# A fused attention and two-expert-layer kernel: background steps of the weights spread by phase, and four PSUM banks for one product

## The chip, the cores and the metric

The kernel runs on one core of a Trainium2 chip. The metric is the device time of one execution in microseconds (us). TensorE (PE) has two levels of clock here, 1.2 and 2.4 GHz; the profile gives the granted share of the higher one. VectorE is called DVE, ScalarE ACT; SP only issues DMAs here.

## The reference

```python
kv  = einsum('bhsd,bhse->bhde', k, v)            # 4 batches, 8 heads, 576 tokens, head size 64
o   = einsum('bhsd,bhde->bhse', q, kv)
x   = o / sqrt(mean(o*o) + 1e-6) * g             # -> 2304 tokens x 512

p   = domain_probs / domain_probs.sum(-1)        # first layer: 4 experts, every token in every one
for e in range(4):
    out += p[:, e] * (relu(x @ w1[e]) @ w2[e])   # 512 -> 1024 -> 512

logits = out @ phi                               # second layer: 8 experts with 4 slots each
d = softmax(logits, over tokens); c = softmax(logits, over slots)
y = c @ [relu((d.T @ out)[e] @ w1'[e]) @ w2'[e] for e in range(8)]
```

All inputs are float32. Most of the arithmetic is the first layer: two products for each of 4 experts over 2304 tokens.

## The kernel before, in words

The 2304 tokens are 18 tiles of 128. Tiles make chunks: chunk 0 is tiles 0 to 3, chunk 1 tiles 4 to 7, and so on, the last one with two tiles. Chunks 0 and 1 are group 0 and go through experts 0, 1, 2, 3 first; chunks 2 to 4 then go through experts 3, 2, 1, 0. The change touches group 0.

A float32 matrix is held as two float16 halves, hi and lo (`split`, L615: ACT writes hi at L618 with a scale, DVE writes lo = scaled source - hi at L620), and each product is three matmuls, hi*hi, hi*lo and lo*hi. The first product of a chunk (`mm1`, L908) goes by seven products of 2x2 block operands instead of eight, so the weight operands include differences of blocks, T1 to T4, made on DVE (L655). The second product has two forms: plain (`mm2`, L979, one PSUM bank of 128x512 per tile, at the end of a tile one DVE instruction at L1004 scales the bank and adds it to the running sum) and fast (`mm2_fast`, L1011, again seven products, with sums of 128x256 pieces added at L1045). The fast form needs differences of the hidden activations (lines 837 to 886; they are queued by `fast_h` and worked off about one a step by `work_off`, L819) and of w2's blocks (made at L738, `prep_t2`).

For experts 1 and 2 in group 0 (`SOON`) an expert has four phases: first product of chunk 0 (plain), first product of chunk 1 (feeding the fast form), plain second product of chunk 0, fast second product of chunk 1. Expert 0 is plain throughout and goes chunk by chunk.

The order of instructions is written out by hand. `main` is a list of steps (12 matmuls of 256 columns or 6 of 512 each); a first product has 14 steps, chunk 0's second 16, chunk 1's fast second 14. Beside each step, `run_bg` (L1366) takes steps from background chains. A chain has a start, an end and a list of steps, and gives each main step a weight: 1, or W1 = 0.55 for a step of a first product, and 0 for the two steps before a second product and its first step (`CALM`). Its steps are dealt out in proportion. Two chains matter here. In phases of expert e - 1, `prep_w1` and `prep_w2` prepare expert e: four size steps on ACT (L541) for w1, then `scale_steps` (a reduce and a small diagonal matrix on DVE at L548 and L553, empty steps, a tiny matmul `ar_w` on PE at L561, small DVE steps), 15 steps of splits and differences of w1, then the same for w2 with 9 steps of splits. `prep_t2` prepares w2's differences of the expert itself, with 8 differences at L738 and 8 splits, in two batches that are also written to DRAM.

PSUM has eight banks in four pools of two: `ps_x`, `ps_o`, `ps_yz`, `ps_a`. A step of the main list names its pool: in chunk 0's second product of experts 1 and 2 all four tiles take turns on the two banks of `own` (`ps_x`), while `other` (`ps_o`) is lent to the background's small matmuls; chunk 1's fast product that follows starts its products 1 and 7 in the two banks of `ps_o`.

SP issues the DMAs of its own queue in program order; an input page is loaded when a page is free and not claimed, at most ten at a time (`pump`, L169).

Of the kernel before, what the change touches and what calls it, by code (L numbers as in the profile page):

```python
# [43 lines left out]
W1 = 0.55  # L44
# [3 lines left out]
def attn_moe_softmoe_kernel(ctx: ExitStack, tc: tile.TileContext, qT, k, v, g, dp, w1, w2, phi, m1, m2a, m2b, out):  # L48
# [442 lines left out]
    def pe(f):  # L491
        after[0].append(f)
# [25 lines left out]
    def attn_steps(cs, eng, stride=6):  # L518

        ps_ = [p for c in cs for p in pairs(c)]  # L520
        st = [[] for _ in range(stride * (len(ps_) - 1) + len(pair_steps(ps_[0], eng)))]
        for i, p in enumerate(ps_):
            for j, f in enumerate(pair_steps(p, eng)):
                st[i * stride + j].append(f)
        return [lambda fs=fs: [f() for f in fs] for fs in st]
# [19 lines left out]
    def w_scale_a(e, nm, act=False):  # L545
        m = wmx.pop((e, nm))
        a = small.tile([128, 1], F32, tag=f"am{nm}", name=f"am_{nm}_{e}")
        nc.vector.tensor_reduce(out=a, in_=m, axis=AX.X, op=ALU.add)  # L548
        dg = work.tile([128, 128], F32, tag="dgw", name=f"dg_{nm}_{e}")
        if act:  # L550
            nc.scalar.activation(dg, gdiag, AF.Copy, scale=a)
        else:
            nc.vector.tensor_scalar(  # L553
                out=dg, in0=gdiag if nm == "w1" else ident, scalar1=a, scalar2=None, op0=ALU.mult
            )
        war[e, nm] = dg

    def w_spread(e, nm, bank=ps_a, between=lambda: None):

        ps = bank(f"ar_{nm}_{e}")  # L560
        nc.tensor.matmul(ps[:, 0:128], ones, war[e, nm], start=True, stop=True)  # L561
        between()
        r = war[e, nm] = small.tile([128, 1], F32, tag=f"ar{nm}", name=f"ar_{nm}_{e}")
        nc.vector.tensor_reduce(out=r, in_=ps[:, 0:128], axis=AX.X, op=ALU.add if nm == "w1" else ALU.max)

    def scale_steps(e, nm):

        return [lambda: w_scale_a(e, nm), lambda: None, lambda: None, lambda: pe(lambda: w_spread(e, nm)),
                lambda: w_scale_b(e, nm)]

    def w_scale_b(e, nm, between=lambda: None):
# [185 lines left out]
    def prep_w2(g_, e):  # L757
        raw = lambda b: need(("w2", g_, e, b))
        st = []
        if g_ == 0:  # L760
            st += [lambda b=b: w_size(e, "w2", b) for b in range(4)]
            st += scale_steps(e, "w2")

        def sp(b, i, part):
            w2_split(e, b, b, i, part)

        bi = [(b, i) for b in (0, 2, 1, 3) for i in range(2)]
        return st + stagger(
            [lambda b=b, i=i: sp(b, i, 0) for b, i in bi], [lambda b=b, i=i: sp(b, i, 1) for b, i in bi]
        )  # L770
# [501 lines left out]
    is1 = []  # L1272
# [15 lines left out]
    for e, seq in runs:  # L1288
        if True:
            for n, (gi, which, c) in enumerate(seq):  # L1290
                ei = EXP[gi].index(e)
                wk = (0 if e == KEPT else gi, e)
                last = gi == 1 and ei == E - 1
                kept = gi == 0 and e == KEPT
                soon = gi == 0 and e in SOON
                fast = c != 0 if e == KEPT or soon else gi == 1 and not (last and c == DISP[-1])
                turns = gi == 1 or e == KEPT or soon

                own, other = (ps_x, ps_o) if n % 2 == 0 else (ps_o, ps_x)
                ch = CH[c]  # L1300
                marks[f"mm{which}", gi, e, c] = len(main)
                done = not kept and not any(i == which for g_, i, _ in seq[n + 1:])
                if which == 1:
                    if not turns:
                        own, other = ps_x, ps_o
                    st = [lambda wk=wk, c=c, u=u, P=P, fast=fast, bank=own: mm1(wk, c, u, P, fast, bank)
                          for P in ORDER for u in range(2)]
                    if not fast:
                        st[0] = lambda c=c, f=st[0]: (start_chunk(c), f())
                    if ei == E - 1:  # L1310
                        st[-1] = lambda c=c, f=st[-1]: (f(), x_drop(c))
                    if done:
                        st[-1] = lambda wk=wk, f=st[-1]: (f(), [pg.release() for pg in wop[wk].values()])
                    if not fast:
                        st[-1] = lambda f=st[-1]: (f(), flush())
                elif fast:
                    st = [lambda wk=wk, c=c, P=P, j=j, bank=own, ei=ei: mm2_fast(wk, c, P, j, bank, ei == 0)
                          for P in ORDER3 for j in range(len(ch) // 2)]
                    st[-1] = lambda wk=wk, c=c, f=st[-1]: (f(), end_fast(wk, c))
                    if done:  # L1320
                        st[-1] = lambda wk=wk, f=st[-1]: (f(), [pg.release() for pg in w2p[wk].values()])
                else:

                    tu = [(ch[0], 0), (ch[1], 0), (ch[0], 1), (ch[1], 1)] + [(t, u) for t in ch[2:] for u in range(2)]
                    st = [
                        lambda wk=wk, c=c, t=t, u=u, kk=kk, ei=ei, b=own if soon else ps_o:
                        mm2(wk, c, t, u, kk, ei == 0, b)
                        for t, u in tu for kk in range(2)
                    ]
                    if last and done:  # L1330

                        st = []
                        for u in range(2):
                            for kk in range(2):
                                st += [
                                    lambda wk=wk, c=c, t=t, u=u, kk=kk, b=(ps_w if t in ch[2:] else ps_o):
                                    mm2(wk, c, t, u, kk, False, b) for t in ch
                                ]
                                st[-1] = lambda wk=wk, c=c, u=u, kk=kk, f=st[-1]: (
                                    f(), hbuf[c][2 * u + kk].release(), w2p[wk][2 * kk + u].release()  # L1340
                                )
                    else:
                        st[-1] = lambda c=c, f=st[-1]: (f(), end_chunk(c))
                        if done:
                            st[-1] = lambda wk=wk, f=st[-1]: (f(), [pg.release() for pg in w2p[wk].values()])
                main += st
                is1 += [which == 1] * len(st)
                lend += [other if which == 1 or fast or soon else ps_w] * len(st)
                marks["end" if which == 2 else "mm1end", gi, e, c] = len(main)


# [8 lines left out]
    def chain(start, stop, steps, claim=0, w1=W1):  # L1360
        assert start < stop
        hooks.setdefault(start, []).append(lambda: (
            chains.append([start, stop, deque(steps), w1, 0.0, []]), claims.__setitem__(0, claims[0] + claim)
        ))

    def run_bg(now):  # L1366

        for ch in chains:
            start, stop, steps, w1, credit = ch[:5]
            wt = [(w1 if is1[i] else 1.0) * calm[i] for i in range(now, stop)]  # L1370
            if not wt:
                n = len(steps)
            else:
                credit += wt[0] * (len(steps) - credit) / max(sum(wt), 1e-3)
                n = min(int(credit + 1e-6), max(1, -(-len(steps) // len(wt))))
                ch[4] = credit - n
            for _ in range(min(n, len(steps))):
                for f in ch[5]:
                    f()
                ch[5].clear()  # L1380
                after[0] = ch[5]
                steps.popleft()()
# [15 lines left out]
    chain(6, m["mm2", 0, 0, 0], w2s[4:-4], 4)  # L1398
    chain(m["mm2", 0, 0, 0] - 2, m["mm2", 0, 0, 0] + 4, w2s[-4:])
    chain(10, m["mm1", 0, 0, 1], attn_steps([1], nc.vector), 3 + 6, 1.0)  # L1400
    for e in range(1, E):
        chain(m["mm2", 0, 0, 0] + 12 if e == 1 else m["mm1", 0, e - 1, 0], m["end", 0, e - 1, 1] - 1,
              prep_w1(0, e, V) + prep_w2(0, e), 12 if e == 1 else 6)
    def claim(at, n):
        hooks.setdefault(at, []).append(lambda: claims.__setitem__(0, claims[0] + n))

# [6 lines left out]
    chain(m["end", 0, E - 1, 1] + 3, m["end", 1, E - 1, 2], disp_steps(1), 2, 1.0)  # L1413
    for e in FAST:
        if e in SOON:
            chain(m["mm1", 0, e, 0] + 2, m["mm2", 0, e, 1] - 2, prep_t2(e, V), 2)
        else:
            chain(m["mm1", 1, E - 1, 4], m["mm2", 1, E - 1, 4], prep_t2(e, V), 4)
            gate["w2", 1, e] = m["mm1", 1, E - 1, 4] - 6
        gate[e] = m["mm1", 1, e + 1, 3]  # L1420
# [435 lines left out]
```

## Time and profile before

| | us |
|---|---|
| three runs | 824.14, 824.60, 825.47 |
| profiled execution, its own time | 825.78 |
| its span, first to last instruction | 824.0 |
| PE busy | 801.3 (97%) |
| DVE busy | 571.2 (69%) |
| ACT busy | 398.5 (48%) |
| mean granted PE clock | 0.993 |

The span is what the trace covers; 1.8 us of the execution's time lie around it. Matmuls are pipelined, so PE's busy time says only that it seldom waits; the shares of DVE and ACT are means over stages that differ.

### The profile page before, as it was taken

What the parts mean: (1) busy time and instruction counts of PE and PEld (TensorE: products, weight loads), DVE (VectorE), ACT (ScalarE), POOL (GpSimd) and SP (SyncE); (2) the same over time, 40 slices, a digit from 0 to 9 for tenths busy, and PEclk for the clock granted to TensorE, in tenths of its full rate; (3) what the DMA queues carried; (4) which work ended last, traced back from release to release, by engine and by line L of the source; (5) the groups of instructions that cost most, each with busy time, mean ns of one, the idle gap of its engine ahead of it and who ended that gap; (6) DMA issues with size and microseconds to landing.
All of it is one profiled execution on the core that took longest, in us unless ns stands there. A gap on an engine that the chain in (4) does not pass through costs nothing.

```text
span 824.0 us, 17838 instructions
## 1 busy us (share of the span) xinstructions
PE 801.3 (97%) x7558; PEld 644.8 (78%) x7558; DVE 571.2 (69%) x1139; ACT 398.5 (48%) x784; POOL 5.9 (1%) x13
## 2 busy tenths in 40 slices
PE   8999999999999999999999999999999999999996
PEld 8876668658855876878888888898889888984545
DVE  6997967987798557769969727874578537742403
ACT  5876756555655333774656536241444125421203
POOL 0000000000000000000000000000000000000000
PEclk9999999999999999999999999999999999999998
DMA  9951540277228600110012860044103252669697
GB/s 361 403 238 50 198 189 27 77 258 264 102 68 287 248 28 1 51 29 2 1 52 85 306 251 1 1 181 141 66 1 115 92 204 82 227 226 362 216 395 234
DMA packets 40753, 126.03 MB, mean 153 GB/s; under 512 B 4066, under 2 KB 11106, under 8 KB 40674
## 3 DMA queue, kind: packets, MB, share of 16 engines
q1 hardware_dynamic: 40016, 124.57, 41.6%
q8 instruction: 59, 0.97, 0.5%
q10 hardware_dynamic: 658, 0.33, 0.1%
q14 instruction: 20, 0.16, 0.1%
HBM read 96.57 MB, written 28.31 MB: 152 GB/s over the span
## 4 chain that ended last, share of the span: by engine, by line
PE 83%; DVE 13%; ACT 2%; issue 2%; DVEq 0%; POOL 0%; ACTq 0%; POOLq 0%
PE p L929 33%; PE m L1029 25%; PE y L992 13%; DVE pages L620 3%; PE s L1705 2%; PE o L339 2%; PE so L1735 2%; PE keep L264 1%; DVE pages L946 1%; DVE t L959 1%; PE kv L284 1%; PE x2T L1062 1%; DVE pages L738 1%; DVE pages L844 1%; PE xT L408 1%
## 5 line engine op out<-in xcount | busy, mean ns | idle before, releaser
L929 PE MATMUL p<-pages 128*128 128x256 f16 (+1 forms) x3360 | 339.4, 262 | 1.5 <-DVE kvs L308 1.0
L929 PEld LDWEIGHTS <-pages 128*128 128x128 f16 x3360 | 300.0, 98 | 34.7 <-issue 2.1
L1029 PE MATMUL m<-pages 128*128 128x256 f16 x2016 | 224.7, 273 | 2.3 <-DVE pages L1045 2.3
L1029 PEld LDWEIGHTS <-pages 128*128 128x128 f16 x2016 | 196.9, 98 | 26.8 <-issue 3.9
L992 PE MATMUL y<-pages 128*128 128x512 f16 x576 | 132.0, 386 | 5.4 <-DVE pages L1004 4.6
L992 PEld LDWEIGHTS <-pages 128*128 128x128 f16 x576 | 56.9, 100 | 72.4 <-issue 10.6
L1045 DVE SCALAR_TENSOR_TENSOR pages<-m,pc,pages 128x256 f32<-128x256 f32 x148 | 65.8, 480 | 63.1 <-PE m L1029 62.6
L618 ACT ACTIVATE pages<-pages,s_w 128x512 f16<-128x512 f32 (+1 forms) x113 | 79.4, 740 | 20.9 <-DVE s_w L594 16.0
L620 DVE SCALAR_TENSOR_TENSOR pages<-pages,s_w 128x512 f16<-128x512 f32 (+1 forms) x113 | 85.1, 778 | 3.1 <-ACT pages L618 2.8
L839 ACT CAST pages<-t 128x512 f16<-128x512 f32 (+1 forms) x84 | 46.5, 557 | 57.5 <-DVE t L882 24.1
L848 DVE TENSOR_TENSOR pages<-t,pages 128x512 f16<-128x512 f32 (+1 forms) x84 | 50.5, 608 | 2.5 <-ACT pages L839 1.3
L837 ACT ACTIVATE pages<-pages 128x512 f16<-128x512 f32 (+1 forms) x56 | 31.9, 569 | 35.6 <-DVE pages L871 19.1
L959 DVE TENSOR_TENSOR t<-p,t 128x512 f32<-128x512 f32 x36 | 24.7, 689 | 25.7 <-PE p L929 25.5
L839 ACT CAST pages<-pages 128x512 f16<-128x512 f32 (+1 forms) x28 | 15.6, 558 | 53.3 <-DVE t L886 53.3
L945 ACT ACTIVATE pages<-t 128x512 f16<-128x512 f32 x36 | 22.6, 628 | 30.1 <-DVE t L959 29.8
L867 DVE TENSOR_TENSOR t<-p,t 128x512 f32<-128x512 f32 (+1 forms) x28 | 17.1, 613 | 26.2 <-PE p L929 25.2
L871 DVE TENSOR_TENSOR pages<-p,pages 128x512 f32<-128x512 f32 (+1 forms) x28 | 17.1, 612 | 25.5 <-PE p L929 25.5
L541 ACT ACTIVATE junk<-pages 128x1024 bf16<-128x1024 f32 x32 | 33.8, 1055 | 2.2 <-DMA pages<-in_w 1.8
L954 ACT COPY t<-p 128x512 f32<-128x512 f32 x36 | 20.8, 579 | 28.4 <-PE p L929 28.4
L844 DVE SCALAR_TENSOR_TENSOR pages<-pages 128x512 f16<-128x512 f32 (+1 forms) x56 | 33.1, 608 | 0.9 <-ACT pages L837 0.5
L861 ACT COPY t<-p 128x512 f32<-128x512 f32 (+1 forms) x28 | 14.5, 525 | 39.4 <-PE p L929 39.4
L946 DVE SCALAR_TENSOR_TENSOR pages<-t,pages 128x512 f16<-128x512 f32 x36 | 24.6, 684 | 1.1 <-ACT pages L945 0.7
(184 smaller groups left out, 699.0 us busy)
## 6 DMA issues: line engine op xcount, KB each, us to landing
pages<-in_w SPq DMA_DIRECT2D x48, 512.0 KB, 4.6
o<-pages SPq DMA_DIRECT2D x33, 512.0 KB, 7.6
pages<-o SPq DMA_DIRECT2D x33, 512.0 KB, 6.1
pages<-in_m SPq DMA_DIRECT2D x32, 512.0 KB, 5.3
pages<-in_m2a SPq DMA_DIRECT2D x16, 512.0 KB, 5.3
pages<-in_m2b SPq DMA_DIRECT2D x16, 512.0 KB, 10.1
o_t<-pages SPq DMA_DIRECT2D x12, 512.0 KB, 5.0
pages<-o_t SPq DMA_DIRECT2D x12, 512.0 KB, 5.4
```

What stands on the lines that cost most here:

```text
L541: nc.scalar.activation(junk, src, AF.Square if nm == "w1" else AF.Abs, accum_out=m[:, b:b + 1])
L618: nc.scalar.activation(dst[:, 0], src, AF.Copy, scale=s)
L620: nc.vector.scalar_tensor_tensor(out=dst[:, 1], in0=src, scalar=s, in1=dst[:, 0], op0=ALU.mult, op1=ALU.subtract)
L839: nc.scalar.copy(dst, sh(src))
L844: nc.vector.scalar_tensor_tensor(out=h[:, 1], in0=sh(src), scalar=0.0, in1=h[:, 0], op0=ALU.max, op1=ALU.subtract)
L848: nc.vector.tensor_tensor(out=h[:, 1], in0=sh(src), in1=h[:, 0], op=ALU.subtract)
L929: nc.tensor.matmul(ps[:, fp * n:fp * n + n], l, r, start=(fp + i == 0 and P in first), stop=(fp == 1 and i == len(mms) - 1 and P in end), ...
L946: late.append(lambda: nc.vector.scalar_tensor_tensor(out=hl, in0=src, scalar=0.0, in1=hh, op0=ALU.max, op1=ALU.subtract))
L959: nc.vector.tensor_tensor(out=t, in0=ps, in1=t, op=ALU.add)
L992: nc.tensor.matmul(ps, a, b, start=(u + kk + fp + i == 0), stop=(u == 1 and kk == 1 and fp == 1 and i == 2))
L1029: nc.tensor.matmul(ps, l, r, start=(i == 0 and j == 0 and P in (1, 2, 7)), stop=(i == len(mms) - 1 and j == nh - 1 and P in (2, 3, 4)), sk ...
L1045: nc.vector.scalar_tensor_tensor(out=x, in0=src, scalar=pc, in1=x, op0=ALU.mult, op1=ALU.add)
```

## The change

Three edits. The small matmul of a scale comes one background step later (one more empty step, for w1 and for w2). In chunk 0's plain second product of experts 1 and 2, tiles 0 and 1 take banks of `own` and tiles 2 and 3 of `other`, and nothing is lent to the background in that phase. The background chains of experts 1 and 2 get a weight for each of the four phases, in place of the 0.55 and 1: the next expert's preparation 0.5, 0.1, 0.5, 1.0 (that of expert 1, within expert 0, keeps the old weights), the expert's own w2 differences 0.25, 0.45, 0.3, 0.3.

```diff
     def scale_steps(e, nm):
-        return [lambda: w_scale_a(e, nm), lambda: None, lambda: None, lambda: pe(lambda: w_spread(e, nm)),
+        return [lambda: w_scale_a(e, nm), lambda: None, lambda: None, lambda: None, lambda: pe(lambda: w_spread(e, nm)),
                 lambda: w_scale_b(e, nm)]
...
-                        lambda wk=wk, c=c, t=t, u=u, kk=kk, ei=ei, b=own if soon else ps_o:
+                        lambda wk=wk, c=c, t=t, u=u, kk=kk, ei=ei, b=(own, other)[t // 2 % 2] if soon else ps_o:
                         mm2(wk, c, t, u, kk, ei == 0, b)
...
-                lend += [other if which == 1 or fast or soon else ps_w] * len(st)
+                lend += [other if which == 1 or fast else None if soon else ps_w] * len(st)
...
-            wt = [(w1 if is1[i] else 1.0) * calm[i] for i in range(now, stop)]
+            wt = [(w1(i) if callable(w1) else w1 if is1[i] else 1.0) * calm[i] for i in range(now, stop)]
...
+    def by_phase(e, *ws):
+        at = [m["mm1", 0, e, 0], m["mm1", 0, e, 1], m["mm2", 0, e, 0], m["mm2", 0, e, 1]]
+        return lambda i: ws[sum(i >= a for a in at[1:])]
+
     for e in range(1, E):
         chain(m["mm2", 0, 0, 0] + 12 if e == 1 else m["mm1", 0, e - 1, 0], m["end", 0, e - 1, 1] - 1,
-              prep_w1(0, e, V) + prep_w2(0, e), 12 if e == 1 else 6)
+              prep_w1(0, e, V) + prep_w2(0, e), 12 if e == 1 else 6,
+              W1 if e == 1 else by_phase(e - 1, 0.5, 0.1, 0.5, 1.0))
...
-            chain(m["mm1", 0, e, 0] + 2, m["mm2", 0, e, 1] - 2, prep_t2(e, V), 2)
+            chain(m["mm1", 0, e, 0] + 2, m["mm2", 0, e, 1] - 2, prep_t2(e, V), 2, by_phase(e, 0.25, 0.45, 0.3, 0.3))
```

## Rows read from the trace of the kernel before

**Rows 1.** The page: busy us, share of the span, instructions.
```profile
PE 801.3 (97%) x7558; PEld 644.8 (78%) x7558; DVE 571.2 (69%) x1139; ACT 398.5 (48%) x784; POOL 5.9 (1%) x13
```
**Rows 2.** PE's waits: line waiting <- line awaited, total us, times, longest.
```profile
PE y L992 <- DVE pages L1004: 4.6, 2, 2.3
...
PE ar_w L561 <- DVE pages L946: 1.3, 2, 0.6
...
PE y L992 <- DVE pages L946: 0.8, 1, 0.8
...
PE ar_w L561 <- DVE dg_w L553: 0.3, 1, 0.3
```
**Rows 3.** PE over expert 1: start us, us, count, wait before and its releaser.
```profile
135.13 0.49 PE L561 MATMUL ar_w<-dg_w,ones 128*128 128x128 f32 x2 [0.65 <-DVE pages L946]
...
153.79 10.52 PE L992 MATMUL y<-pages 128*128 128x512 f16 x48
166.61 12.21 PE L992 MATMUL y<-pages 128*128 128x512 f16 x48 [2.29 <-DVE pages L1004]
178.65 5.40 PE L1029 MATMUL m<-pages 128*128 128x256 f16 x48
```
**Rows 4.** Busy us by stretch: length, PE, PEld, DVE, ACT, POOL, clock, DMA.
```profile
153.79:166.55 12.76, 10.53 (x50) 4.70 (x48) 12.57 (x21) 6.75 (x13) 0.00 (x0) 1.00 0.04 4
166.55:178.65 12.10, 12.04 (x48) 5.12 (x48) 11.43 (x19) 10.31 (x19) 0.00 (x0) 0.86 0.61 203
...
167.00:168.00 1.00, 1.00 (x4) 0.41 (x3) 1.00 (x3) 0.84 (x2) 0.00 (x0) 0.52 0.96 369
```
**Rows 5.** PE in group 1, after another wait.
```profile
396.56 2.78 PE L1029 MATMUL m<-pages 128*128 128x256 f16 x24 [1.58 <-DVE pages L1045]
```
**Rows 6.** Busy us by stretch, after the waits of rows 3 and rows 5.
```profile
136.00:138.00 2.00, 2.00 (x21) 1.79 (x19) 1.90 (x7) 0.58 (x1) 0.00 (x0) 1.00 0.22 90
...
398.00:400.00 2.00, 2.00 (x21) 1.80 (x19) 2.00 (x5) 0.00 (x0) 0.00 (x0) 1.00 0.00 0
```
**Rows 7.** DVE over expert 1's second product of chunk 0.
```profile
154.00 0.69 DVE L844 SCALAR_TENSOR_TENSOR pages<-pages 128x512 f16<-128x512 f32 x1 [0.16 <-ACT pages L837]
...
156.60 1.23 DVE L655 TENSOR_TENSOR pages<-pages 128x1024 f32<-128x1024 f32 x1
157.74 0.69 DVE L738 TENSOR_TENSOR pages<-pages 128x512 f32<-128x512 f32 x1
158.34 0.69 DVE L848 TENSOR_TENSOR pages<-t,pages 128x512 f16<-128x512 f32 x1
158.94 0.75 DVE L620 SCALAR_TENSOR_TENSOR pages<-pages,s_w 128x512 f16<-128x512 f32 x1
159.61 0.68 DVE L738 TENSOR_TENSOR pages<-pages 128x512 f32<-128x512 f32 x1
...
165.81 0.74 DVE L1004 SCALAR_TENSOR_TENSOR pages<-y,pc,pages 128x512 f32<-128x512 f32 x1
...
179.42 0.16 DVE L548 TENSOR_REDUCE am_w<-mx_w 128x1 f32<-128x4 f32 x1 [1.43 <-ACT junk L541]
...
180.41 0.74 DVE L1004 SCALAR_TENSOR_TENSOR pages<-y,pc,pages 128x512 f32<-128x512 f32 x1
```
**Rows 8.** DVE where expert 0's last second product begins.
```profile
94.75 0.74 DVE L620 SCALAR_TENSOR_TENSOR pages<-pages,s_w 128x512 f16<-128x512 f32 x1
...
96.02 1.47 DVE L946 SCALAR_TENSOR_TENSOR pages<-t,pages 128x512 f16<-128x512 f32 x2
```
**Rows 9.** SP's queue over expert 1: start us, us, DMAs.
```profile
144.48 30.01 SPq L163 DMA_DIRECT2D pages<-in_w  x7
174.54 0.90 SPq L240 DMA_DIRECT2D o_t<-pages  x2
...
179.92 17.43 SPq L163 DMA_DIRECT2D pages<-in_w  x5
```
**Rows 10.** The page's DMA issues: size, median us from issue to landing.
```profile
pages<-in_w SPq DMA_DIRECT2D x48, 512.0 KB, 4.6
```
**Rows 11.** ACT, the last of w2's four size steps.
```profile
178.24 1.05 ACT L541 ACTIVATE junk<-pages 128x1024 bf16<-128x1024 f32 x1
```

## The prediction

> **What bounds the kernel now.** First the page: PE is busy for 801.3 of 824.0 us, DVE and ACT far less [rows 1]. So only two things can pay: PE's waits, some 23 us in all, and time in which its clock is low. Next the list of PE's waits: the largest of the steady part is 4.6 us, two waits of plain second-product matmuls for L1004, the DVE instruction that empties a bank; there are 1.3 us of the small matmul `ar_w` behind DVE's L946, 0.8 us of second-product matmuls behind L946, and 0.3 us of `ar_w` behind the diagonal matrix of L553 [rows 2]. Then PE in order of time. In expert 1 `ar_w` waits 0.65 us at the seam of the first two phases, and chunk 0's second product stands 2.29 us exactly half-way, after tiles 0 and 1 [rows 3]; expert 2 has the same pattern, so the totals of [rows 2] are twice one expert's.
>
> The same rows hold a second cost. The first 48 matmuls took 10.52 us, the 48 after the wait 12.21 [rows 3]. The windows say why: clock 1.00 in the first half, 0.86 in the second, 0.52 in the microsecond that begins at 167 [rows 4]. PE stood still for 2.29 us and then ran at its 1.2 GHz level for a while. That costs 12.21 - 10.52 = 1.69 us more, so the stop is worth 2.29 + 1.69 = 3.98 us an expert. The shorter waits have no such price: after 0.65 us [rows 3] and even after 1.58 us [rows 5] the clock reads 1.00 [rows 6].
>
> Why the wait: tile 2 needs tile 0's bank. Tile 0 is complete after 6 of 16 steps of 10.35 / 8 = 1.294 us (10.52 less 0.16 of the last matmul's modelled tail), at 7.8 us from the phase's start at 153.79; DVE empties its bank only at 165.81 [rows 7], at 12.0. DVE is not slow there, it is full: 12.57 of 12.76 us [rows 4].
>
> **The change part by part.** Prices from neighbouring starts in [rows 7]: a split's lo half 159.61 - 158.94 = 0.67 us, a w2 difference or a piece of hidden-activation work 0.60, a w1 difference 1.14, emptying a bank 0.66 (estimate, as a split: 0.74 against 0.75 long).
>
> *Where the background steps fall.* I dealt them out by `run_bg`'s rule. The weights of the next expert's preparation sum over the four phases (with the calm steps left out) to 7.7, 6.6, 13 and 12 before, 42 steps on them: 8, 7, 14, 13. After, 7, 1.2, 6.5 and 12, 44 steps: 11, 2, 11, 20. For w2's differences, 26 steps: 6.6, 6.6 and 13 before, some 6, 7, 13; after 3, 5.4 and 3.9, some 6, 12, 8. So all four differences of the second batch (0.60 each) leave chunk 0's second product for the phase before it; three w1 splits, one w1 difference and the small DVE steps of w1's scale leave that earlier phase.
>
> *DVE up to tile 0's bank.* Before: 8 pieces of hidden work 4.80, 5 splits 3.35, one large difference 1.14, 4 small ones 2.40: 11.7 us from 154.00, which is 165.7 against the 165.81 of the row, so the count holds. After: 8 pieces, 6 splits, one large difference: 9.96 us. DVE starts the phase no later than now (the phase before it gets some 1.6 us lighter in all, but its last two pieces wait for PE's last product): bank 0 is emptied from 10.2 on. Two banks would then still leave a wait of half a microsecond; with tile 2 in `ps_o`, whose banks chunk 1's first product left long ago, it goes wholly, and the clock stays up. Gain 3.98 us an expert, 7.96 in all.
>
> *What is late next.* Tiles 2 and 3 now hold the two `ps_o` banks in which the fast product starts its products 1 and 7. Go on with the sum: bank 1 after 0.66 + 4 splits 2.68 + 2 pieces 1.20, from 14.7; bank 2 after 0.66 + 3 splits 2.01 + 4 pieces 2.40, from 19.8 to 20.5; bank 3 after 2 splits 1.34 and 3 pieces 1.80, from 23.6 to 24.2. PE ends the phase at 16 x 1.294 = 20.7 and starts product 1: bank 2 is just free. Product 7 starts two steps of 1.31 us later (48 matmuls of this product take 5.40 less 0.16 [rows 3]), at 23.3, and needs bank 3. That is a new wait of 0.9 us by the sum; I take 0.6, since the lighter phase before should hand over some 0.3 us earlier, and keep 0 and 1.9 as ends (1.9: the 1.3 us of splits not done in time). Cost 1.2 us in all, at full clock, as after the waits of [rows 6].
>
> *The heavier last phase.* It gets one w1 split and all of w2's size steps, and the 8 w2 splits fall on its last five steps before the end: 5.4 us plus two pairs of additions, about 7 in 6.5, so less than a microsecond is carried into the next expert, whose first addition comes two steps later. DVE's reduce at L548 waits for ACT's sizes (now 1.43 us [rows 7]) with product 6's additions queued behind it, and PE needs those at the ninth step, 31 us from the start of chunk 0's second product. ACT's four sizes of 1.05 us [rows 11] follow its last hidden work at about 22.5, so they end near 27: nothing, with 4 us to spare.
>
> *SP.* The pages decide: w1's pages come free later, so the fourth w2 page is loaded in the fast phase, after both writes of w2 differences, not before them. Those writes wait for splits that end near 14 us of the phase, and a load lands 4.6 us after issue [rows 10]: near 20, needed near 25. The queue runs ahead of PE even now: loads that the list places at the end of one phase go out while it waits for pages [rows 9].
>
> *The size product one step later.* For w1 it leaves the seam for the eleventh step of the first phase and takes a free `ps_o` bank instead of one that L946 still reads; its diagonal matrix is four steps old by then. The waits of 0.65 us go, 1.3 in all. At the start of the kernel the extra step puts `ar_w` behind a main step of 12 matmuls: 0.29 us gone (bounds 0 and 0.3). In expert 0 two extra steps push one split past the end of chunk 1's first product; DVE's last L946 there [rows 8] comes 0.67 us earlier and the 0.80 us wait shrinks to about 0.15: 0.65 (bounds 0 and 0.8).
>
> **Sum.** 7.96 + 1.30 + 0.29 + 0.65 - 1.20 = 9.0 us. The profiled execution took 825.78, so 816.8 by its measure; the median of the runs is 1.2 lower, and I say 815.6.
>
> **The rivals.**
>
> *The wait moves to product 7 and stays long.* For it: DVE still has 24 us of work in a phase of 20.7, and the same bank discipline applies two steps on. Against it: 1.7 us of work leave before bank 0. With a wait of 1.9 us at full clock the time is 815.6 + 2 x 1.3 = 818.2; if the clock then drops as after the 2.29 us wait, 2 x 1.69 more, 821.6.
>
> *Short stops cost clock too.* A kernel that hands a product from bank to bank has a small stop at every seam; if such a stop of 0.6 us already brought the 1.2 GHz level for as long as now, the cost would be 2 x 1.69: 819.0. Against it stand both windows of [rows 6]. The Trainium skill, TensorE: Matmul & The Clock Gate, section "A second HAM failure mode: psum-queue depth-cycling", says that cycling through banks can give micro-idles that make the clock go down and up; by that rule the time would be this rival's, and the trace agrees with it only for the long stop of [rows 4].
>
> *The change doesn't do what it says:* the weights leave DVE's backlog as it is and only the banks differ. Bank 3 was empty at 180.41 + 0.74 [rows 7], 27.4 us after the phase's start; product 7 would wait until then, 4.0 us instead of 2.29, and lose the clock as now: 2 x 1.7 lost against 2.2 gained at the small waits, 827 by the profiled execution and 826 for the median.
>
> *Slower: ACT's sizes starve.* The late w2 page comes behind loads that wait for pages, in the second batch of [rows 9], which runs from 26 to 43.6 us of the phase's start. In its middle, at 35, the page lands near 39.6, the last size ends at 40.7, DVE stands at L548 until then with the additions behind it, and PE waits from 31: 9.7 + 1.7 us of clock, twice: 815.6 + 22.8 = 838. It decides from a landing about 29 us after the phase's start; the page it takes is one whose last split ends near 14, which speaks against it.
>
> **How the numbers follow.** Forecast 0.63, longer wait at product 7 0.20, clock lost at short stops 0.07, backlog unchanged 0.06, starved sizes 0.04. The forecast's own range is 814.2 (no wait at product 7, all small waits gone) to 817.5; to leave no more than 2 in 10 out the range is 814.0 to 820.5. What differs by less than 0.2%, 1.6 us, can't be told from no change. The first three cases are faster, all but the tail: 0.88; same 0.07; slower 0.05.
>
> **What would show it.** In the changed kernel's waits the line of y behind L1004 should be gone or below 0.3 us, `ar_w` behind L946 gone; the two halves of chunk 0's second product should be one run of 96 matmuls in 20.7 us at clock 1.00; a wait of m in the product after it, behind L1004, of 0 to 1.9 us should be new. DVE's four L1004 of expert 1 should start near 10, 15, 20 and 23.6 us into the phase. Wrong would be: a clock below 1.00 in these phases, a wait of more than 2 us behind L1045 or L1004 in the fast product, or DVE idle behind ACT's L541 for over 4 us.

## The result, and the profile after

The changed kernel takes 816.67 us (median of 4 runs, 816.39 to 816.95) against 825.04 for the kernel before in the same set: a ratio of 0.9899 (95% interval 0.9882 to 0.9916), 8.4 us faster. 815.6 was forecast, with 814.0 to 820.5 as the range. The profiled execution took 816.95 us with a span of 815.2; profile against profile the gain is 825.78 - 816.95 = 8.83.

PE's waits in the changed kernel (columns as in [rows 2]; p is a bank of a first product, y of a plain second product, m of a fast one):

```profile
PE m L1029 <- DVE pages L1045: 2.3, 2, 1.6
PE m L1029 <- DVE pages L1004: 1.7, 2, 0.9
...
PE y L992 <- DVE pages L946: 0.3, 1, 0.3
```

The 4.6 us of y behind L1004 and the 1.3 us of `ar_w` behind L946 of [rows 2] are gone, the 0.8 us of expert 0 are 0.3, `ar_w` no longer waits for L553, and 1.7 us of m behind L1004 are new, 0.86 for each expert. The first line is group 1's and was there before. In order of time, over expert 1 (compare [rows 3]):

```profile
115.21 14.57 PE L929 MATMUL p<-pages 128*128 128x256 f16 x132
129.62 0.39 PE L561 MATMUL ar_w<-dg_w,ones 128*128 128x128 f32 x2
...
152.11 20.88 PE L992 MATMUL y<-pages 128*128 128x512 f16 x96
172.83 2.78 PE L1029 MATMUL m<-pages 128*128 128x256 f16 x24
176.48 6.71 PE L1029 MATMUL m<-pages 128*128 128x256 f16 x60 [0.86 <-DVE pages L1004]
...
192.42 14.57 PE L929 MATMUL p<-pages 128*128 128x256 f16 x132
```

Chunk 0's second product is one run of 96 matmuls, product 1 follows without a stop, and product 7 (after 24 matmuls) has the new wait. The windows of that product and of what follows the new wait (columns as in [rows 4]):

```profile
176.48:178.00 1.52, 1.52 (x14) 1.36 (x14) 1.39 (x3) 1.49 (x3) 0.00 (x0) 1.00 1.05 410
178.00:180.00 2.00, 2.00 (x21) 1.79 (x19) 0.70 (x2) 1.73 (x4) 0.00 (x0) 1.00 1.01 410
152.11:172.83 20.72, 20.72 (x98) 9.37 (x96) 20.62 (x32) 13.49 (x23) 0.00 (x0) 1.00 0.39 132
```

The clock is 1.00 throughout, after the 0.86 us too. DVE is still full, 20.62 of 20.72 us. Its four emptyings of a bank, and what follows (compare [rows 7]):

```profile
162.32 0.74 DVE L1004 SCALAR_TENSOR_TENSOR pages<-y,pc,pages 128x512 f32<-128x512 f32 x1
...
166.84 0.75 DVE L1004 SCALAR_TENSOR_TENSOR pages<-y,pc,pages 128x512 f32<-128x512 f32 x1
...
171.89 0.74 DVE L1004 SCALAR_TENSOR_TENSOR pages<-y,pc,pages 128x512 f32<-128x512 f32 x1
...
175.68 0.75 DVE L1004 SCALAR_TENSOR_TENSOR pages<-y,pc,pages 128x512 f32<-128x512 f32 x1
...
180.09 0.15 DVE L548 TENSOR_REDUCE am_w<-mx_w 128x1 f32<-128x4 f32 x1
```

They start 10.2, 14.7, 19.8 and 23.6 us after the phase's start at 152.11, the very numbers of the prediction's sum. The reduce at L548 waits for nothing.

Where the 8.8 us of span come from is read from the starts of the phases. Those of before that are not in [rows 3]:

```profile
115.98 18.50 PE L929 MATMUL p<-pages 128*128 128x256 f16 x168
...
197.21 18.50 PE L929 MATMUL p<-pages 128*128 128x256 f16 x168
...
247.84 12.21 PE L992 MATMUL y<-pages 128*128 128x512 f16 x48 [2.29 <-DVE pages L1004]
```

| | before | after | gain | forecast |
|---|---|---|---|---|
| up to expert 1 | 115.98 | 115.21 | 0.77 | 0.94 |
| its two first products | 153.79 - 115.98 = 37.81 | 152.11 - 115.21 = 36.90 | 0.91, twice 1.82 | 1.30 |
| chunk 0's second product | 178.65 - 153.79 = 24.86 | 172.83 - 152.11 = 20.72 | 4.14, twice 8.28 | 7.96 |
| chunk 1's fast product | 197.21 - 178.65 = 18.56 | 192.42 - 172.83 = 19.59 | -1.03, twice -2.06 | -1.20 |
| sum | | | 8.81 | 9.00 |

Expert 2 shows the same waits. Nothing is lost or won after expert 2. Of the first row the change itself gained 1.02: the profiled execution of the changed kernel was already 0.25 us behind at 35 us, before anything that was edited (a run of matmuls that starts at 35.34 before starts at 35.59 after). A stop costs some 0.17 us more than its wait: a wait is counted from the modelled end of the last matmul, the stop from the time at which the next could have started (166.61 - 153.79 - 10.35 = 2.47 for the 2.29).

### The profile page after: what moved, and what is told of

Same layout as the page of the kernel before. It is cut to its first block, busy times and chain, and to the rows that moved or that the text cites. A ratio compares the mean times of both kernels' runs of the same rounds, so it can differ in the third digit from the quotient of the medians.

```text
span 815.2 us, 17828 instructions
## 1 busy us (share of the span) xinstructions
PE 797.4 (98%) x7558; PEld 643.6 (79%) x7558; DVE 570.2 (70%) x1139; ACT 399.1 (49%) x784; POOL 5.9 (1%) x13
## 4 chain that ended last, share of the span: by engine, by line
PE 78%; DVE 16%; ACT 3%; issue 2%; DMA 0%; DVEq 0%; POOL 0%; SPq 0%; ACTq 0%; POOLq 0%
PE p L929 31%; PE m L1029 24%; PE y L992 10%; DVE pages L620 4%; PE s L1711 2%; PE o L339 2%; DVE pages L848 2%; PE keep L264 2%; PE so L1741 1%; PE kv L284 1%; DVE pages L655 1%; DVE pages L946 1%; DVE pages L844 1%; PE x2T L1062 1%; DVE t L959 1%
## 5 line engine op out<-in xcount | busy, mean ns | idle before, releaser
L992 PE MATMUL y<-pages 128*128 128x512 f16 x576 | 128.3, 380 | 0.3 <-DVE pages L946 0.3
L1045 DVE SCALAR_TENSOR_TENSOR pages<-m,pc,pages 128x256 f32<-128x256 f32 x148 | 65.8, 480 | 60.1 <-PE m L1029 59.5
L837 ACT ACTIVATE pages<-pages 128x512 f16<-128x512 f32 (+1 forms) x56 | 31.9, 569 | 37.7 <-DVE pages L871 19.0
L837 ACT ACTIVATE pages<-t 128x512 f16<-128x512 f32 (+1 forms) x28 | 15.8, 570 | 21.0 <-DVE t L867 21.0
## 6 DMA issues: line engine op xcount, KB each, us to landing
pages<-in_m2b SPq DMA_DIRECT2D x16, 512.0 KB, 10.2
```

The costliest lines, as they stand in the source:

```text
L837: nc.scalar.activation(dst, sh(src), AF.Relu)
L992: nc.tensor.matmul(ps, a, b, start=(u + kk + fp + i == 0), stop=(u == 1 and kk == 1 and fp == 1 and i == 2))
L1045: nc.vector.scalar_tensor_tensor(out=x, in0=src, scalar=pc, in1=x, op0=ALU.mult, op1=ALU.add)
```

## The experiments

The three edits were put in by themselves and taken out, the new wait and the clock were tried apart, and one kernel goes on from the change. Ratios, with their 95% intervals, are to the kernel before on the same chip: experiments 1, 2, 4 and 8 ran beside 15 runs of it with a median of 824.46 us, experiments 3, 5, 6 and 7 on another chip beside 17 with a median of 825.67. The kernel before itself differs by 1.2 us between these sets, so across sets the ratios and the traces are compared.

**1. The banks alone.** The kernel before with

```diff
-                        lambda wk=wk, c=c, t=t, u=u, kk=kk, ei=ei, b=own if soon else ps_o:
+                        lambda wk=wk, c=c, t=t, u=u, kk=kk, ei=ei, b=(own, other)[t // 2 % 2] if soon else ps_o:
-                lend += [other if which == 1 or fast or soon else ps_w] * len(st)
+                lend += [other if which == 1 or fast else None if soon else ps_w] * len(st)
```

> The kernel before with the bank edit alone: tiles 2 and 3 of chunk 0's second product in ps_o, old weights, no extra step. Theory (DVE's backlog sets the wait, banks only move it): the wait of 2.3 us between tiles 1 and 2 goes, but DVE empties bank 2 only at 23 us of the phase and bank 3 at 27.4, as before, so product 1 of the fast product waits some 2.2 us for bank 2 at 20.7, the clock falls, and product 7 waits up to 1.7 more: 824 to 827 us, no gain. Rival (four banks are what the change gains by): both waits and the clock's fall go, 8 us less, 817.

Measured: 826.07 us against 824.46, ratio 1.0017 (1.0008 to 1.0026): slightly slower. PE in order of time:

```profile
154.08 20.88 PE L992 MATMUL y<-pages 128*128 128x512 f16 x96
177.13 4.22 PE L1029 MATMUL m<-pages 128*128 128x256 f16 x24 [2.16 <-DVE pages L1004]
181.50 2.85 PE L1029 MATMUL m<-pages 128*128 128x256 f16 x24
...
258.37 2.78 PE L1029 MATMUL m<-pages 128*128 128x256 f16 x24 [2.16 <-DVE pages L1004]
262.74 2.78 PE L1029 MATMUL m<-pages 128*128 128x256 f16 x24 [1.59 <-DVE pages L1004]
```

The wait of 2.29 us is gone from the middle of y and stands as 2.16 us at product 1. In expert 1 DVE has emptied banks 2 and 3 at 23.0 and 27.4 us of the phase (its last two L1004 start at 176.33 and 180.70), just as expected. The clock falls there behind the wait (product 1 takes 4.22 us in place of 2.78, granted clock 0.63), and DVE catches up meanwhile; in expert 2 it doesn't fall, and product 7 waits 1.59 us more. The banks alone only choose where PE pays for DVE's backlog.

**2. All but the banks.** The changed kernel with those lines as before.

> The changed kernel without the bank edit: all four tiles in ps_x, new weights and the extra step kept. Theory (the weights do it): DVE has emptied bank 0 near 11.0 us of the phase, tile 2 could start at 10.35, so there is one wait of about 0.6 us behind L1004 in y and none at product 7, whose banks nobody holds; clock 1.00; 816.4 us, the same as the whole change within 0.5. Rival (the banks are needed): a wait of 1.5 us or more in y with the clock falling, 819 to 822.

Measured: 816.14 us, ratio 0.9901 (0.9886 to 0.9916), as fast as the whole change.

```profile
152.10 10.52 PE L992 MATMUL y<-pages 128*128 128x512 f16 x48
163.11 10.52 PE L992 MATMUL y<-pages 128*128 128x512 f16 x48 [0.49 <-DVE pages L1004]
173.47 9.33 PE L1029 MATMUL m<-pages 128*128 128x256 f16 x84
...
192.03 14.57 PE L929 MATMUL p<-pages 128*128 128x256 f16 x132
```

One wait of 0.49 us with two banks, none at product 7. With the backlog shortened, the bank edit trades 0.49 us in y for 0.86 us at product 7: in these profiles the two second products of an expert take 192.03 - 152.10 = 39.93 us without it and 192.42 - 152.11 = 40.31 with it.

**3. The weights alone.** The kernel before with `by_phase` and the two chains' weights.

> The kernel before with the new weights alone. Theory: as the changed kernel without its bank edit (816.1), plus 0.8 us for the two small waits that the extra step takes away: 816.9; that is nearly the whole gain. Rival: the three edits need each other, 819 or more.

Measured: 817.27 us, ratio 0.9906 (0.9887 to 0.9925). The same 0.49 us in y, no wait of `ar_w` at the seam, and 0.80 us of expert 0 back. This edit is nearly the whole gain.

**4. The later size product alone.** The kernel before with the one empty step more.

> The kernel before with the extra empty step in scale_steps alone. Theory: the wait of 0.29 us of ar_w at the start goes, the 0.80 us wait of expert 0 falls to about 0.3, and ar_w of experts 2 and 3 comes one main step after the seam, when L946 has read its bank: 0.29 + 0.47 + 1.3 = 2.1 us less, 822.7. Rival (these waits come back at the next use of DVE): 824 to 825.

Measured: 821.88 us, ratio 0.9964 (0.9952 to 0.9977), 2.6 us faster where 2.1 was expected; the interval holds both. Both waits of `ar_w` behind L946 and the one behind L553 are gone; PE's waits now open with the first line here, and the others show the second halves of y in experts 1 and 2:

```profile
PE y L992 <- DVE pages L1004: 5.0, 2, 2.5
...
165.10 12.21 PE L992 MATMUL y<-pages 128*128 128x512 f16 x48 [2.48 <-DVE pages L1004]
...
245.62 10.52 PE L992 MATMUL y<-pages 128*128 128x512 f16 x48 [2.48 <-DVE pages L1004]
```

PE arrives at chunk 0's second product 1.70 us earlier than before (152.09 against 153.79), tile 2 starts only 1.51 us earlier (165.10 against 166.61): 0.2 us an expert are given back there (2.48 for 2.29).

**5. All but the later size product.**

> The changed kernel without the extra empty step: new weights and banks. Theory: the 0.30 us at the start and the 0.47 us of expert 0 come back, ar_w of experts 2 and 3 stays clear of the seam through the weights alone, product 7 waits 0.9 us: 816.7 + 0.8 = 817.5. Rival (the step is what moves ar_w off the seam): 1.6 more, 819.

Measured: 817.88 us, ratio 0.9913 (0.9896 to 0.9931), 1.2 us above the whole change's median where 0.8 was expected; those medians are of different sets, and by the traces the step is worth 1.0: from the run of matmuls near 35 us to expert 1 it is 115.67 - 35.02 = 80.65 here and 115.21 - 35.59 = 79.62 in the changed kernel. `ar_w` of experts 2 and 3 has no wait: once the weights are there, the step buys only the small waits of the start and of expert 0, where PE waits 0.80 us again. Alone it bought 2.6; the edits overlap at the seam.

**6. PE kept at work through the stop.** The kernel before with

```diff
+                    if soon:
+                        st[8] = lambda f=st[8]: (keep(11, psA.tile([128, 512], F32, tag="a", name="fill"), identh,
+                                                      identh.unsqueeze(1).to_broadcast([128, 4, 128])), f())
```

> The kernel before with 11 matmuls of the identity (128x512 float16, 2.4 us together, into a spare ps_a bank that nobody reads) on PE ahead of tile 2 in chunk 0's second product of experts 1 and 2, so that PE works through the time in which it stood for the bank. Theory (the clock falls because PE stands): the wait is as long as before but the clock stays 1.00 in both halves; the time is that of an execution of the kernel before in which neither stop brings the clock down, 822.3 us, and its spread shrinks. Rival (the slow second half has another cause, as the DMA traffic that begins there): it stays slow and the time stays at 824.5.

Measured: 822.67 us, ratio 0.9970 (0.9957 to 0.9984).

```profile
153.49 10.52 PE L992 MATMUL y<-pages 128*128 128x512 f16 x48
163.85 2.54 PE L264 MATMUL fill<-identh 128*128 128x512 f16 x11
166.30 10.52 PE L992 MATMUL y<-pages 128*128 128x512 f16 x48
```

Tile 2 begins as late as before, but its 48 matmuls take 10.52 us, not the 12.21 of [rows 3], while the DMAs of that stretch go on (201 GB/s, 203 in [rows 4]). Expert 2 shows the same. As a low clock doesn't follow every stop (experiment 7), one profile would prove little, but the runs agree: ten of the twelve lie between 821.99 and 823.27 us, with a mean granted clock of 0.996 to 0.998, while 16 of the 17 of the kernel before lie at 823.68 or above. So it is the standing that costs clock, and work that nobody needs saves it: 2 to 3 us for the two experts. The other two of the twelve took 824.81 and 825.07 us at a mean clock of 0.994; no trace shows where they lost it.

**7. The kernel before once more, for a profile.**

> The kernel before, unchanged. Its 15 runs so far lie at 822.3, between 824.1 and 825.0, and between 825.2 and 825.9: steps of about 1.7 us. Theory: each of the two 2.3 us stops brings the clock down in some executions only, so a profile whose time is in the middle group shows the low clock after one stop alone, and one near 825.8 after both. Rival: the low clock follows both stops always, and the groups have another cause.

Measured: 824.91 us. In expert 1 and in expert 2:

```profile
167.44 12.21 PE L992 MATMUL y<-pages 128*128 128x512 f16 x48 [2.28 <-DVE pages L1004]
...
248.67 10.52 PE L992 MATMUL y<-pages 128*128 128x512 f16 x48 [2.29 <-DVE pages L1004]
```

Equal stops, and only the first was followed by a low clock. In the profile that the prediction read, both were. With 1.69 us less for one fall and 0.84 us more for a later opening, 825.78 gives 824.93. (The opening: the 54 matmuls of `keep` at the start of the kernel took 8.44 us in place of 7.69, and the products began 0.84 us later. So the groups of times are not the clock's at the stops alone.)

**8. The fast product in the banks of tiles 0 and 1.** The changed kernel with

```diff
-                own, other = (ps_x, ps_o) if n % 2 == 0 else (ps_o, ps_x)
+                own, other = (ps_x, ps_o) if (n % 2 == 0 or soon and n == 3) != (soon and e == SOON[-1]) else (ps_o, ps_x)
```

> The changed kernel with the fast second product in the two banks that tiles 0 and 1 used (and the pools exchanged for expert 2, so that its first product does not meet them). Theory (the new wait of 0.86 us at product 7 is bank 3 and nothing else): the wait goes from both experts, 1.7 us less than the whole change, 815.0. Rival (DVE's backlog is paid in any case): as much comes back as a wait of product 6 behind L1045, 816.7.

Measured: 814.62 us (median of 4), ratio 0.9884 (0.9870 to 0.9897), 2.1 us below the changed kernel's median. The two are of different sets and their ratios' intervals overlap, so the traces must tell.

```profile
153.00 20.88 PE L992 MATMUL y<-pages 128*128 128x512 f16 x96
173.72 9.33 PE L1029 MATMUL m<-pages 128*128 128x256 f16 x84
...
192.28 14.57 PE L929 MATMUL p<-pages 128*128 128x256 f16 x132
```

No wait at product 7 and none in its place: PE's waits list no L1004 at all, and L1045 with group 1's 2.3 us as before. An expert's second products take 192.28 - 153.00 = 39.28 us, 1.03 less than in the changed kernel and 0.65 less than without the bank edit. (This execution came to expert 1 later than that of the changed kernel, by waits before 20 us, where the edit changes nothing.) It is the fastest kernel here. In this kernel the four banks paid once the next product no longer wanted the last two.

## Why the prediction was right, and where it was off

*What bounds the kernel* was read rightly: stops of PE for a bank that a full DVE empties late, with the clock as a second cost. Experiments 1 to 3 show that DVE's backlog is the cause: more banks move the stop, and less work ahead of the banks shortens it to 0.49 us with the banks as they were. Experiment 6 shows that the clock falls because PE stands.

*Where the background steps fall, and DVE up to the banks:* the sum by the rule of `run_bg` and prices from neighbouring starts gave the four bank times to a tenth of a microsecond, and the trace has the counts that the sum used between the banks (4 splits and 2 pieces, 3 and 4, 2 and 3). Dealing the steps out by hand was worth more than DVE's busy share, which hardly moved (20.62 of 20.72 us).

*The new wait* was named with its place, and its sum, 0.9 us, was right (0.86). The 0.3 us that I took off for a lighter phase before did not come. DVE's first piece did start earlier, 0.02 us after the phase's start (at 152.13) in place of 0.21 [rows 7], but the work up to bank 0 then took 10.19 us and not 9.96, so bank 0 was emptied at 10.2 all the same. Nor did DVE wait there for PE's last product, as the prediction says: what it waited for before was ACT's L837 [rows 7]. The missed allowance is 0.5 us for two experts, 0.9 with what a stop costs beside its wait.

*The bank edit* was credited with more than it gave. The prediction's own numbers, half a microsecond of wait with two banks against 0.6 to 0.9 at product 7 with four, already say that it buys nothing here; experiment 2 measured 0.49 against 0.86.

*The seam and expert 0:* the seam was undersized (1.82 for 1.30, since a stop costs more than its wait), and put down to the extra step, while the weights alone remove it too (experiments 3 and 5). The start was undersized as well (some 0.55 for 0.29), expert 0 overestimated (0.33 us of its wait stay where 0.15 were expected).

*The close sum is partly luck.* 9.00 and 8.81 differ by 0.19, but the table's rows miss by -0.17, +0.52, +0.32 and -0.86 us and cancel.

*The last step of the sum failed.* By the profiled execution 816.8 was forecast and 816.95 came. I then took off 1.2 us because the median of the runs lay that far below the profile of before. But that profile had the low clock after both stops, and as experiment 7 shows, other executions have it after one: part of the 1.2 us was the very cost that the sum removes, and it was removed twice. The changed kernel's profile lies 0.28 us above its median. That is 0.9 of the 1.07 us by which 815.6 missed.

*The rivals.* The wait stayed neither long nor did it take the clock. That short stops cost clock too is refuted for stops up to 1.59 us. The Trainium skill (TensorE: Matmul & The Clock Gate, "A second HAM failure mode: psum-queue depth-cycling") tells of a kernel that cycles through banks and whose micro-idles between groups of matmuls made the clock go down and up; the traces here agree with it for stops of 2.2 to 2.5 us only, and there in five of eight. Banks without weights were tried in experiment 1: 826.07 where the rival said 826, though by another way, since product 1 waits before product 7 does, which the rival had missed. Of the starved sizes nothing was seen: the fourth size ends 27.6 us after the phase's start, near 27 as estimated.

*What was not settled:* the two chains' weights were not tried apart. By the prediction's count it is w2's differences that free bank 0 (2.40 us leave, one more split of 0.67 comes), but no run shows it. The bank edit's small cost inside the change stands in the traces (39.93 against 40.31 us an expert) and not in the times, whose ratios are equal (0.9901 and 0.9899).

## What to carry to other kernels

Where one engine stands for another that is full, first shift the full engine's work out of the stretch before the deadline; more buffers alone moved the stop to the next user of the buffers (experiment 1). Follow a bank to the product that takes it next before lending it. And before a profile is scaled to a median, look whether the profile holds a cost that comes in some executions only.

## What was not expected of the hardware

The clock's fall after a stop is not certain. Stops with waits of 2.16 to 2.48 us were followed by the 1.2 GHz level five times and not followed by it three times: in [rows 3] and at 247.84 both times, in experiments 1, 4 and 7 in expert 1 and not in expert 2. Where it fell in y, 48 matmuls of 512 columns took 12.21 us in place of 10.52; in m, 24 of 256 columns took 4.22 in place of 2.78. After waits of 0.49, 0.65, 0.86, 1.58 and 1.59 us it was 1.00 each time. Eleven matmuls that nobody needs, 2.45 us from the first to the start of tile 2, kept it at 1.00 through both stops of the profiled execution.
